# Another order table for a fused linear-attention and gated feed-forward kernel on one core

## The chip, the cores and the metric

The kernel runs on one core of a Trainium2 chip. A core has TensorE (PE, matrix products into PSUM), VectorE (DVE), ScalarE (ACT) and GpSimd (POOL), which run side by side, each through its own instructions in their order, and SyncE (SP), which issues DMAs; POOL and ACT issue DMAs as well. The metric is the device time of one execution in microseconds (us); lower is better.

## The reference

The program first does a linear attention with exponential features for 8 batches of 8 heads (576 positions, head size 64, 128 features), then a feed-forward layer over the 4608 rows of 512 that come out.

```python
def phi(x):
    proj = np.einsum('bhsd,df->bhsf', x, w_phi)
    proj = proj - np.max(np.abs(proj), axis=-1, keepdims=True)
    return np.concatenate([np.exp(proj), np.exp(-proj)], axis=-1)
q_p, k_p = (phi(q), phi(k))
kv = np.einsum('bhsf,bhsd->bhfd', k_p, v)
z = np.sum(k_p, axis=2)
num = np.einsum('bhsf,bhfd->bhsd', q_p, kv)
den = np.einsum('bhsf,bhf->bhs', q_p, z)[..., None] + 1e-06
...
x = np.ascontiguousarray(attn_out.transpose(0, 2, 1, 3)).reshape(B * S, H * D)
...
gate = np.maximum(x @ w_gate, 0.0)
val = x @ w_val
return (gate * val @ w_out).astype(np.float32)
```

## The kernel before

The work is first described as 2,077 numbered steps with their dependencies, and then issued in an order that is written out by hand as text, the table `ORDER`.

**Attention of a batch.** K is turned so that head size lies on partitions (`turn_pe` on TensorE for batches 0 and 1, `turn_dma` as a transposing DMA on SP's queue for the others). For each pair of heads (`k_item`, line 379) TensorE projects K, DVE takes the largest absolute value, ACT makes the two exponentials and the scale of each row, and POOL multiplies V by the scale (`scale`). `k_kv` (line 468) sums the products of features and scaled V in 20 small matmuls, and ACT or DVE copies the sum out ("kv copy"). For Q, `q_cols` projects, DVE takes the maximum and ACT the exponentials; `q_num` (line 585) makes numerator and denominator in three groups of heads (6, 6 and 4 matmuls), DVE combines them and takes the reciprocal, POOL divides, and the result is turned into `xT`, the feed-forward input: by TensorE with a copy by ACT or DVE for batches 0 and 1 ("xT copy"), by a transposing DMA after that. The last 64 positions of each batch are handled in pairs of batches.

**Feed-forward.** `ffn` (line 655) runs for nine groups of 512 rows: for each of 12 slices of the inner dimension, 4 matmuls with w_val, a copy by ACT, 4 matmuls with w_gate, and one DVE instruction that rectifies and multiplies. Then three times 4 matmuls with w_out for each of 4 row tiles, a copy, and a store from SP's queue. Group 0 belongs to batch 0 and is cut into parts of 128, 128 and 256 rows. Group 8 holds the left-over positions (`xT_mix`), and its last two stores are issued by ACT.

**What fixes the order.** Each entry of `ORDER` is a step's number, a letter for its engine (P for TensorE, A for ACT, D for DVE, G for POOL, S for SP) and one figure for each buffer or PSUM bank that the step is the first to use. `1397P5` issues step 1397 on TensorE and puts its result in PSUM bank 5. Some steps may run on ACT or on DVE; the letter chooses. `w21` and `z9` issue fillers (21, 9): matmuls of a zero tile that nobody reads (`warm`, line 198). Every engine runs its entries in the order of the table; semaphores enforce the dependencies. All fillers stand in the first part.

From batch 2 on, transposing DMAs (turns) and POOL's loads are kept apart: a turn waits for the last load that the table has ahead of it, and the first load after turns waits for the last turn (`read`, line 67).

```python
if o.alone and e == SP:
    o.gate, last_turn = last_load, o
if o.alone and e == POOL:
    o.gate, last_turn = last_turn, None
if o.bytes and e == POOL:
    last_load = o
```

Steps named later: 42, 196, 200 and 202 are copies of turned K (42 and 202 of the left-over rows); 98 is a kv copy and 153 an xT copy of batch 0; 270P projects Q of batch 1; 1397P and 1415P are feed-forward steps of group 0. 10S, 16G, 17G, 18G, 20G, 25G and 26G are early loads (a quarter of k; the two halves of q; two pieces of w_val; the left-over rows of v, and q, both of batch 1), 66G, 56G and 76G the scalings of V for batch 0. 711G and 1182G load v for batches 4 and 7 (711G its left-over rows), 708G left-over rows of k; 531G and 857G load left-over rows of v; 712S, 533S and 1185S turn K, 1188S turns Q, 816S turns a chunk of feed-forward input. 717P and 1190P project K of batches 4 and 7. 1983S stores a tile of group 7; 2056 is a copy of group 8, 2058S and 2069S are stores of it.

Of the kernel before, what the change touches and what calls it, by code (L numbers as in the profile page):

```python
# [1016 lines left out]
0G 4D 8S 7S 9S 1S 14S0 3D 10S 5G 6S w21 35P00 w1 33P1 13S0 36A w1 37P2 16G0 34A 2D 15S 38A w2  # L1017
57P340000 25G1 47P561111 59A 61D 67P012222 69A 48D 12S 17G 51D 11S 49A w13 41P20 22G0 68D 60A 50A
58D 18G 54A 52A w9 39P5 42D 63A 71D 23G0 w1 87P3000 40D 89A 72A 88D w8 77P25333 62A 81D 53A w4
43P40 64A 78D 74A 65A 90A 44D 91A6 73A 66G 92D 83A 93D w10 115P3 70A 116D0 79A 94D 75A w11 45P4  # L1020
84A1 80A 26G1 119P0 85D 55A 86D 108P3601 82A 56G 111A w2 103P25 105A 46D w5 113P1 112A 120D w2
134P4 104A 101P60 76G 135D1 107A 117P0 138P2 102A 114D 97P41 110A 118D 95P72 139D 21G 132P6 121A0
193P11 96A 98D 106A 127P0223 19G 133D 136P7 129A 137D 20G 109A 194D 130A z9 141P40000 29G 99P53
142D 147P61 24G1 195P7 100A 148D 131A 143D z3 144P32 122P15 196A 145D 160P41110 149D 128A 146D z3
157P21 161D 126A 197P7 150D 217P633433 158D 151G 124A 162D 154P02 159D 123A 155D z2 207P420504 198A
156D 199P1 163D 223A 218D 164G 125A 221D 220A 28G 211D z11 165P00 140A1 222A 152P7 170P50220 208D
219A 27G0 201P31 153D 200A 167P61 171D 1359P70 166A 168D 173P12 172D 31G 1360A 1363P01 169D 1375P72
174D 203P51 175D 1376A 202D 1364A 183P61010 210A 180P11 204D 247P71110 186P02 209A 1377P3 184D
1387P53 213A 187D 205P4 181D 224A 188D 212A 176D 1378D0 1361P0 177G 182D 1388A 249A 237P231015 185D
1383P52 189D 250A 206D 1365P1 190G 1385P6 1384A 243A 248D 178P5 239A 1362D z3 191P4 179D 242A  # L1030
277P70010 1366D 192D 240A 227P512220 1386D 279A 1371P40 241D 1391P61 283A 228D 1393P3 1372A 1392A
278D 1379P42 251A 252A 1373P6 254G 1380A 1374D 230A 1389P4 1394D 1381P6 232A 1390D 30G 1399P30 229A
1367P41 1382D 231D 280A 1403P53 225A 1400A 281D 1405P6 226G 234A 233A 1369P7 238D 282A 1401P3
1395P12 1404A 1402D 270P2023 1396A 1406D 1368A 1397P5 275A 1407P30 32G 1370D 1415P13 1398D 276A
271D 263P46 1416A 253G 1409P7 1408A 274D 1423P51 235A 265A 1417P1 1410D 214A 1411P32 244A 264D
1424A 236G 347P00 215A 269A 257P74 1418D 348A 1425P5 245D 1435P10 258A 1426D 1451P03 1412A 267D
273A 284P75 216G 1436A 1413P3 268A 259P15 1414D 272A 285D 1443P61 1431P32 1452A 1445P2 288D 260A
1453P0 1444A 246G 286A 1437P1 1446D 291P60 1432A 255P26 1438D 287A 292D 293D 266A 1447P31 1433P1
256D 294A 1449P7 289A 1419P40 1454D 311P60102 1434D 261P27 1448A 1420A 1450D 312D 298P01221 1421P3
262A 1455P13 290A 1422D 301P40 1459P72 313D 1456A 1457P2 302D 1471P31 1460A 299D 1461P5 300D 295P62  # L1040
1472A 1427P10 303D 296D 349P7320 1462D 1428A 297D 1429P0 1458D 350D 1463P42 308P51 304D 314P10
1430D 1464A 1465P6 305G 351A 309D 1473P2 315D 1487P43 316D 1474D 1489P0 310D 1488A 321P11012 352A
1467P20 1490D 324P50 355A 1479P41 306P71 325D 1468A 1439P03 1466D 322D 1441P2 317D 1440A 323D
1475P62 307A 318G 1442D 1469P0 327P11 1476A 1491P73 1470D 1480A 1481P2 353D 340P60222 1492A 1493P4
1477P0 328D 326D 1499P70 383G0 1494D 1482D 1495P53 329D 1478D 1483P41 1501P2 1496A 354A 356P10
1513P0 357D 358D 341D 1485P5 359A 1484A 1508P3 1500A 1486D 330D 331G 334P10 319P4 337P71 1509P 320D
381G1 335D 336D 1503P5 342D 338D 382G1 339D 366P41100 372P12 1518P6 373D 1502D 363P71 1497P2 1519P
1498D 364D 367D 1520P 343D 344G 332P2 1504P 1521A0 333D 365D 1522S 345P6 368D 1514P 346A 375P21
1539P72 386S0 376D 374D 1510P 389S0 1527P41 1505P 388S0 1528A 1540A 360P60 369P12 1506A1 1523P40
361D 387S 370D 1511A0 362D 401P753331 377D 371D 391P362122 390S 1525P2 403A 395D 394A 1515P 393A  # L1050
1507S 1524A 1512S 1535P13 1526D1 1529P4 392D 1536A 397A 411P230403 1530D 1543P10 404A 417A 405D
527G0 1541P4 378D 1544A 402D 396A 385G0 1547P11 414A 408A 431P70001 406A 1537P6 384G0 432D 1548A
1542D 1545P1 433A 532G0 434A 1531P42 1516A1 1546D 528G0 1533P7 1538D 1532A 415D 407A 421P011210
379G 1567P60 412D 416A 422D 435A 418A 529G1 413A 1549P4 409D 398A 424A 1534D 1551P53 423A 1550D
427A 468P32301 436A 447P7012 1552A 425D 437G 1553P4 452A 469D 426A 1569P5 448D 438G 473A 1568A
1555P12 472D 419A 453A 410G 1570D 1563P61 428A 450A 399D 449A 1554D 1557P5 474A 451D 1556A 400G
454P74 461P20 1558D 460A 441P18 1564A 429D 1565P5 462D 457A 420G 442A 1559P60 456A 1566D 467A
1561P1 455D 466A 533S1 458D 471A 439P59 430G 1560A 465D 443P7a 440A 380S0 459A 475P61 1576P0 476D
444A 477D 470A 1562D 482P50010 534S 479P41 463A 494P71222 445P3b 478A 483D 1577P 535S1 480D 446A
484D 464A 481D 485P10 495D 538P633534 486D 537S1 548P542025 487D 1578P 540A 488D 496D 554A 489G  # L1060
491P21 541A 1571P1 492D 1579A0 542D 490S2 509P70100 497P02 1572P 493D 543A 539D 550A 1517S 503P21
510D 1573P 498D 553A 536S 499D 551A 500D 511D 506P62 501G 504D 1581P0 544A 507D 508D 505D 518P71010
502S 515P32 512D 521P61 519D 1582P 513G 520D 516D 1574A1 674S0 558P270301 517D 522D 1583P 560A 523D
524D 549D 561A 514S 525G 568P131412 578P61110 559D 1586P5 580A 552D 526S 581A 1587P 569D 555A 562D
1580S 608P24120 570A 1588P 579D 1575S 564A 572D 563A 531G1 1599P63 582A 609D 574A 1603P72 573A
530G1 1584D0 583A 614A 1601P3 610A 709G0 575A 1607P01 1600A 707G1 545A 571A 1602D0 1605P6 1604A
710G0 1608A 1611P10 1606D 613A 585G 1613P3 556D 1612A 612D 611A 1615P73 584G 1614D 1589A1 565A
594P0630 546A 566D 1616A 601P14 615P25 598D 547G 597A 1609P3 576D 600A 1591P72 599A 1610D 621A
1595P60 567G 1592A 619D 618A 1597P3 595D 1596A 602D 620A 586P73 577G 590P60 603A 587D 596A 1623P51
616D 604A 591D 1625P7 605D 1624A 557G 1598D 592P06 607A 1593P1 606A 593D 711G0 622P60 588P57 623D  # L1070
624D 1619P30 1594D 589A 708G1 625A 632P40220 629P02 1620A 626P51 1627P12 630D 617A 627D 631D 1617P6
# [108 lines left out]
```

## Time and profile before

| | us |
|---|---|
| median of 4 runs | 385.08 |
| lowest and highest run | 383.89 and 387.73 |
| the profiled execution | 383.89 |
| its span, first to last instruction | 382.0 |
| TensorE busy | 371.1 |
| VectorE busy | 263.3 |
| ScalarE busy | 238.1 |
| GpSimd busy | 168.9 |

The profile comes from one execution. An engine's busy time counts each instant once in which one of its instructions ran; a matmul's own duration includes its way through the array, so matmuls that follow each other closely overlap. "Idle before" is the time an engine stood still ahead of an instruction, with what ended it behind an arrow. The span in 40 slices of 9.55 us, in tenths of busy time:

```profile
PE   8798999999999999999999999999999999999994
DVE  5999887558787789877976997679636745432230
ACT  5999975189978946894777478667953304122221
POOL 4885744328836943693397327813651210000000
```

The first four slices hold the attention of batch 0 and part of batch 1's, before there is much feed-forward work to run beside it. The other batches' attention lies beside the feed-forward work of the batches before, up to slice 32, and the rest is feed-forward work alone.

### The profile page before, as it was taken

The numbers are of one execution on the slowest core, as the hardware profiler recorded it, in microseconds if no ns is written. First come the engines' busy times: TensorE is split into PE (matmuls) and PEld (weight loads), VectorE is DVE, ScalarE is ACT, GpSimd is POOL, SyncE is SP. The second block draws the span as 40 slices with busy tenths as digits, with TensorE's granted clock in tenths as the row PEclk, the third lists the DMA queues.
The fourth block names the chain that finished last, engine by engine and source line by source line (L and its number), as shares of the span: only waits on it lengthen the run. The fifth ranks groups of instructions, "written<-read, shape, count | busy, mean of one in ns | idle before, by whom it ended". The sixth has DMA issues, their size and how long they took to land.

```text
span 382.0 us, 8797 instructions
## 1 busy us (share of the span) xinstructions
PE 371.1 (97%) x3376; PEld 207.3 (54%) x3376; DVE 263.3 (69%) x650; ACT 238.1 (62%) x546; POOL 168.9 (44%) x201
## 2 busy tenths in 40 slices
PE   8798999999999999999999999999999999999994
PEld 6577788544654555455546554554455544444452
DVE  5999887558787789877976997679636745432230
ACT  5999975189978946894777478667953304122221
POOL 4885744328836943693397327813651210000000
PEclk9999999999999999999999999999999999999999
DMA  8999794879746948886589559842401031200025
GB/s 211 213 137 252 111 145 58 123 143 237 113 98 184 251 91 143 164 164 106 108 227 143 83 118 202 182 87 30 124 2 44 14 57 55 70 0 0 2 82 138
DMA packets 85609, 45.00 MB, mean 118 GB/s; under 512 B 56672, under 2 KB 79072, under 8 KB 85568
## 3 DMA queue, kind: packets, MB, share of 16 engines
q0 software_dynamic: 32800, 21.83, 35.1%
q1 hardware_dynamic: 52448, 22.42, 26.1%
q8 instruction: 26, 0.43, 0.4%
q10 hardware_dynamic: 320, 0.20, 0.2%
q14 instruction: 15, 0.12, 0.1%
HBM read 37.81 MB, written 9.44 MB: 124 GB/s over the span
## 4 chain that ended last, share of the span: by engine, by line
PE 90%; DVE 3%; ACT 3%; issue 1%; DMA 1%; SPq 0%; POOL 0%; ACTq 0%; DVEq 0%; POOLq 0%
PE ps L669 48%; PE ps L707 25%; PE ps L482 5%; PE ps L600 5%; PE ps L506 2%; PE ps L389 2%; ACT kp L350 1%; DMA wo_sb<-in_k_dram 1%; ACT qp L350 1%; DVE mk L400 1%; DVE qT L328 0%; PE ps L641 0%; PE ps L436 0%; ACT kT L328 0%; PE ps L531 0%
## 5 line engine op out<-in xcount | busy, mean ns | idle before, releaser
L675 ACT CAST val<-ps 128x512 bf16<-128x512 f32 (+2 forms) x132 | 67.3, 531 | 74.2 <-PE ps L669 69.6
L678 DVE SCALAR_TENSOR_TENSOR h<-ps,val 128x512 bf16<-128x512 f32 (+2 forms) x132 | 75.4, 584 | 53.0 <-PE ps L669 38.7
L707 PE MATMUL ps<-wo_sb,h 128*128 128x512 bf16 (+1 forms) x444 | 104.3, 373 | 0.0
L669 PE MATMUL ps<-xT,wv_sb 128*128 128x512 bf16 (+2 forms) x480 | 98.9, 336 | 0.5 <-ACT xT L648 0.2
L669 PE MATMUL ps<-xT,wg_sb 128*128 128x512 bf16 (+2 forms) x480 | 99.0, 336 | 0.3 <-ACT val L675 0.3
L350 ACT ACTIVATE qp<-ps 128x512 bf16<-128x512 f32 x144 | 82.0, 631 | 9.6 <-PE ps L506 8.2
L628 POOL TENSOR_TENSOR xu<-u,r 128x512 bf16<-128x512 f32 x36 | 37.5, 1043 | 108.0 <-DVE r L625 68.8
L350 ACT ACTIVATE kp<-ps 128x512 bf16<-128x512 f32 x128 | 70.5, 616 | 5.0 <-PE ps L389 2.5
L669 PEld LDWEIGHTS <-wg_sb 128*128 128x128 bf16 x528 | 45.8, 98 | 41.5 <-issue 3.6
L669 PEld LDWEIGHTS <-wv_sb 128*128 128x128 bf16 x528 | 45.9, 98 | 40.8 <-issue 2.1
L707 PEld LDWEIGHTS <-h 128*128 128x128 bf16 x444 | 41.3, 98 | 43.4 <-issue 1.8
L415 POOL TENSOR_TENSOR vs<-vn,ek 128x1024 bf16<-128x1024 f32 x31 | 59.0, 1902 | 7.8 <-DVE ek L365 3.5
L400 DVE TENSOR_REDUCE mk<-ps 128x4 f32<-128x512 f32 x64 | 41.6, 676 | 3.7 <-PE ps L389 1.9
L516 DVE TRANSPOSE_TENSOR_REDUCE mq<-ps 128x16 f32<-128x512 f32 x56 | 37.1, 693 | 6.4 <-PE ps L506 4.4
L600 PEld LDWEIGHTS <-qp 128*128 128x128 bf16 x640 | 30.9, 98 | 16.0 <-issue 1.2
L615 DVE TENSOR_TENSOR u<-ps,t 128x195 f32<-128x195 f32 (+3 forms) x120 | 37.4, 329 | 2.0
L600 PE MATMUL ps<-kv,qp 128*128 128x65 bf16 x640 | 35.1, 193 | 0.2 <-ACT kp L350 0.2
L608 DVE TENSOR_TENSOR t<-ps,cq 128x195 f32<-128x195 f32 (+1 forms) x84 | 25.9, 325 | 13.0 <-PE ps L600 9.5
L718 ACT COPY ob<-ps 128x512 f32<-128x512 f32 x20 | 11.6, 597 | 25.6 <-PE ps L707 24.6
L482 PEld LDWEIGHTS <-kp 128*128 128x128 bf16 x512 | 21.7, 98 | 3.7 <-ACT val L675 0.4
L482 PE MATMUL ps<-vs,kp 128*128 128x65 bf16 x512 | 23.3, 193 | 0.1
L482 PE MATMUL ps<-vsm,kpm 128*128 128x65 bf16 x128 | 20.6, 193 | 0.0
(95 smaller groups left out, 317.5 us busy)
## 6 DMA issues: line engine op xcount, KB each, us to landing
out_dram<-ob SPq DMA_DIRECT2D x32, 256.0 KB, 2.5
vn<-in_v_dram POOLq DMA_DIRECT2D x7, 1024.0 KB, 8.7
kn<-in_k_dram POOLq DMA_DIRECT2D x7, 512.0 KB, 6.1
qn<-in_q_dram POOLq DMA_DIRECT2D x7, 512.0 KB, 7.1
wo_sb<-in_moe_w_out_dram POOLq DMA_DIRECT2D x1, 1536.0 KB, 13.0
wo_sb<-in_k_dram SPq DMA_DIRECT2D x4, 256.0 KB, 3.6
vn<-in_v_dram SPq DMA_DIRECT2D x4, 256.0 KB, 4.5
wg_sb<-in_moe_w_gate_dram POOLq DMA_DIRECT2D x2, 512.0 KB, 10.4
```

The costliest lines, as they stand in the source:

```text
L350: nc.scalar.activation(dst(s), ps.t.rearrange("p (c f) -> p c f", f=f), AF.Exp, scale=sign)
L400: nc.vector.tensor_reduce(m.t.rearrange("p (i x) -> p x i", x=2)[:, x], ps.t.rearrange("p (c f) -> p c f", f=F), axis=AX.X, op=ALU.max, ap ...
L415: eng.tensor_tensor(vs.t[:, :, :, 0:D], vn.t[:, 2 * u : 2 * u + 2].rearrange("p h c d -> p (h c) d")[:, :, None, :] .to_broadcast([P, 2 * ...
L482: nc.tensor.matmul(acc[:, hh, s, :], lhsT=lhsT, rhs=rhs, start=(n == 0), stop=(n == 19))
L516: nc.vector.tensor_reduce(mdst(x), ps.t.rearrange("p (h j t) -> p h j t", j=NQ, t=32), axis=AX.X, op=ALU.max, apply_absolute_value=True, a ...
L600: nc.tensor.matmul(ps.t[:, E * (2 * i + s): E * (2 * i + s + 1)], lhsT=qp.t[:, s, h, :], rhs=kv_of[b][h // 2][0].t[:, h % 2, s, :],)
L615: nc.vector.tensor_tensor(u.t[rows, lo : lo + n], ab[:, :, 0], t.t[rows, 0:n], op=ALU.add)
L628: eng.tensor_tensor(xu.t, u.t[:, :, 0:D], r.t.to_broadcast([P, H, D]), op=ALU.mult)
L669: nc.tensor.matmul(ps.t[:, 0:n], lhsT=w[:, dc, P * fi : P * fi + P], rhs=xt()[:, dc, lo:hi], start=(dc == 0), stop=(dc == NDC - 1),)
L675: nc.scalar.copy(val.t[:, 0:n], pv.t[:, 0:n])
L678: nc.vector.scalar_tensor_tensor(h.t[:, fi, lo:hi], pg.t[:, 0:n], 0.0, val.t[:, 0:n], op0=ALU.max, op1=ALU.mult,)
L707: nc.tensor.matmul(ps.t[:, lo:hi], lhsT=h.t[:, fi, P * t : P * t + P], rhs=wo_sb[:, fi, lo:hi], start=(fi == 0), stop=(fi == NFC - 1),)
```

## The change

Only the table is replaced: the same 2,077 steps in another order, with other PSUM banks and buffers, and with 87 fillers in place of 121. Of the steps that may run on either engine, 64 change it: 11 closing feed-forward copies, 9 kv copies, 8 reciprocals of scales, 3 turn copies and 2 xT copies go from ACT to DVE; 10 feed-forward copies, 8 kv copies, 10 scales, 2 turn copies and 1 xT copy go from DVE to ACT. No function changes. The new order came from two annealing passes over the author's timing model, the first for TensorE work placed in the program's early part and the second for the whole; in that model loads land sooner than they did when the old table was made.

```diff
--- before.py
+++ after.py
@@ -1014,138 +1014,138 @@
 
 
 ORDER = """
-0G 4D 8S 7S 9S 1S 14S0 3D 10S 5G 6S w21 35P00 w1 33P1 13S0 36A w1 37P2 16G0 34A 2D 15S 38A w2
-57P340000 25G1 47P561111 59A 61D 67P012222 69A 48D 12S 17G 51D 11S 49A w13 41P20 22G0 68D 60A 50A
-58D 18G 54A 52A w9 39P5 42D 63A 71D 23G0 w1 87P3000 40D 89A 72A 88D w8 77P25333 62A 81D 53A w4
-43P40 64A 78D 74A 65A 90A 44D 91A6 73A 66G 92D 83A 93D w10 115P3 70A 116D0 79A 94D 75A w11 45P4
-84A1 80A 26G1 119P0 85D 55A 86D 108P3601 82A 56G 111A w2 103P25 105A 46D w5 113P1 112A 120D w2
-134P4 104A 101P60 76G 135D1 107A 117P0 138P2 102A 114D 97P41 110A 118D 95P72 139D 21G 132P6 121A0
-193P11 96A 98D 106A 127P0223 19G 133D 136P7 129A 137D 20G 109A 194D 130A z9 141P40000 29G 99P53
-142D 147P61 24G1 195P7 100A 148D 131A 143D z3 144P32 122P15 196A 145D 160P41110 149D 128A 146D z3
-157P21 161D 126A 197P7 150D 217P633433 158D 151G 124A 162D 154P02 159D 123A 155D z2 207P420504 198A
...
-219A 27G0 201P31 153D 200A 167P61 171D 1359P70 166A 168D 173P12 172D 31G 1360A 1363P01 169D 1375P72
-174D 203P51 175D 1376A 202D 1364A 183P61010 210A 180P11 204D 247P71110 186P02 209A 1377P3 184D
...
-1395P12 1404A 1402D 270P2023 1396A 1406D 1368A 1397P5 275A 1407P30 32G 1370D 1415P13 1398D 276A
...
-624D 1619P30 1594D 589A 708G1 625A 632P40220 629P02 1620A 626P51 1627P12 630D 617A 627D 631D 1617P6
-1626D 1628A 633D 628D 644P31102 1621P2 634D 1618D 675P0730 712S0 645D 1622D 641P11 681A 638P50
...
-1085A 1021P22 1785P1 1183G1 1020D 1778A1 1103D 1060A 1046A 1780P3 1028D 1022D 1086A 1182G1 1023D
...
-1795P42 1783D1 1051A 1123A 1187S1 1799P53 1115A 1052G 1121D 1114D 1805P0 1800A 1189S1 1812A 1801P3
...
-1094A 1097P37 1032S0 1130A 1824A 1839P43 1122A 1098A 1188S 1143P01010 1131P10102 1840A 1797P5 1132D
...
-1982A0 2060P 2074D0 2061P 1997A1 1998S 2054P 2062A 2066P 2064S 2047P2 2075S 2063S 2067P 1983S 2055P
-2068D 2070A 2048P 2056A 2049P 2076A 2057S 2069S 2050A 2058S 2051S 2052S
+0G 4D 8S 7S 9S 1S 10S 3D 6S 5G w21 35P00 14S0 w1 33P1 13S0 36A w1 37P2 16G0 34A 2D 38A w2 57P340000
+17G 12S 60A 61D w2 67P561111 39P0 11S 69A 25G1 71D 41P10 15S 70A 40D 42A 72A 22G0 58D w8 47P212222
+63A 87P0000 68D 73A 20G 88D 64A 62A w7 77P56333 23G0 48D 59A w4 43P40 79A 51D 49A 26G1 81D 91A3 53A
+92D 44D 18G 54A 65A 50A 78D w14 45P4 89A 66G 94D 115P2 74A 55A 90A 93D 83A 84A0 46D 80A 75A 56G 85D
+82A w16 108P3501 116D0 97P40 52A 86D 112A 134P6 103P21 98A 111A w2 117P4 135D1 76G 113P0 106A 138P5
+118D 107A 95P61 139D 110A 136P4 119P1 96A 114D w1 101P52 109A 27G0 120D 105A 195P61 132P7 104A 137D
+127P0323 99P13 21G 121A0 102A 196D 131A 133D 141P20000 19G 193P4 100A 122P56 142D 130A 194D 147P71
+24G1 144P12 143D 128A 217P340403 148D 145D 140A1 157P21110 124A 149D 28G 146D 129A 199P7 218D
+160P11 123A 154P02 150D 158D 219A 151G 161D 159D 126A 162D z5 207P522524 155D 222A 29G 200D
...
+169D 202A 197P1 174D 153A 208D 30G z3 186P41000 203P01 198A 175D 187D 165P3 209A 211D 1383P60
...
+1397P1 244A 1400A 263P6423 1416A 245D 234A 270P07 1398D 229A 1417P3 246G 267D 276A 1411P11 1402D
...
+415D 424A 1569P4 427A 412D 437G 416A 422D 1551P51 417A 1570D 531G1 433A 1537P3 425D 1552A 423A
...
+1563P33 414A 1556A 451D 1557P2 457A 1554D 460A 1565P4 419D 428A 459A 1558D 420G 533S1 456A 468P0712
...
+588P75 607A 623D 624D 586P42 1618D 711G0 625A 1624A 590P26 589D 604A 1619P30 587A 591D 1594D
+632P61112 629P11 1620A 626P70 633D 1627P51 630D 634D 631D 675P4210 627D 712S0 638P00222 628D 677A
...
+717P520403 647D 715S 1635P43 657D 648G 1622D 723A 722A 731D 650P00 1633P6 1636A 713S 651D 733A 658D
...
+1670D 1701P2 812D 1700A 813D 797A 864P712120 856G1 1702D 808P50 866A 820P02 1683P41 821D 870A 857G1
...
+807D 823P20 1704A 1685P4 814D 868D 815G 1689P0 824D 869A 905D 825D 1695P32 907A 1690D 816S1 867A
...
+1799P40 1078A 1784S 1066A 1815P73 1800A 1090G 1108A 1113P0330 1120P64 1112A 1792P 1117D 1182G1
...
+1812A 1188S1 1795P20 1125A 1122A 1091P55 1796A 1185S1 1823P02 1098A 1092D 1130A 1123A 1095P46
...
+1840A 1133D 1119A 1145D 1134P00 1149P41 1825P1 1135D 1136D 1150D 1190P520005 1798D 1200P733530
...
+2032A 1982A0 2039P52 2044A 1983S 2041P4 2040A 2071P6 2042D 2029P1 2035P52 2030D 1996P 2046D 2036A
...
+1993S 2054P 2073P 2061P 2066P 2062A0 2067P 2074A 2055P 2063S 2076A 2075S 2068A 2048P 2064S 2070A
+2056D 2069S 2049P 2058S 2057S 2050A 2052S 2051S
```

A line of "..." marks what is left out; the whole table has 132 lines on each side.

## The prediction

> **What bounds the kernel now.** I read the page's busy shares first, then the chain of waits, then busy time by stretches, and last single instructions at the places where the new order differs.
>
> ```profile
> span 382.0 us, 8797 instructions
> PE 371.1 (97%) x3376; PEld 207.3 (54%) x3376; DVE 263.3 (69%) x650; ACT 238.1 (62%) x546; POOL 168.9 (44%) x201
> ...
> PE 90%; DVE 3%; ACT 3%; issue 1%; DMA 1%; SPq 0%; POOL 0%; ACTq 0%; DVEq 0%; POOLq 0%
> ```
>
> TensorE is busy 97% of the span and holds 90% of the chain that ended last. So a change pays only where TensorE waits, or before its first and after its last instruction. The stretches say where (columns: stretch, length, busy time and instructions of PE, PEld, DVE, ACT, POOL, granted clock, DMA share, GB/s):
>
> ```profile
> 0.00:43.60 43.60, 38.12 (x538) 30.33 (x538) 37.81 (x96) 37.72 (x94) 28.48 (x39) 1.00 1.10 190
> 43.60:377.00 333.40, 332.94 (x2841) 176.97 (x2839) 225.51 (x555) 199.91 (x454) 140.42 (x163) 1.00 0.56 108
> 377.00:382.00 5.00, 0.00 (x0) 0.00 (x0) 0.00 (x0) 0.47 (x1) 0.00 (x0) 0.95 0.51 120
> ```
>
> From 43.6 to 377 TensorE is idle for 0.46 us of 333.4: no order can win much there, and a new wait there is paid in full. After it come 5.0 us of tail. In the first 43.6 us PE's 38.1 us busy are misleading, since a short matmul counts about 0.22 us of busy time and the next follows far sooner:
>
> ```profile
> 0.99 2.42 PE L199 MATMUL ps<-zero 128*128 128x128 bf16 x21 [0.99 <-DVE zero L231]
> ...
> 7.64 0.90 PE L199 MATMUL ps<-zero 128*128 128x128 bf16 x13
> ```
>
> Thirteen filler matmuls on zeros take 0.90 us, so (0.90 - 0.22) / 12 = 0.057 us apart. I matched each engine's instructions with the table's entries in order and took the usual time from one TensorE step's start to the next: 0.22 us for a feed-forward step of width 128, 0.86 for width 512, 0.60 for a kv step, 0.19 and 0.13 for the numerator steps. With these, the steps ahead of entry 1397P, which runs at 43.6 us, come to 23.1 us, and 121 fillers x 0.057 to 6.9. The other 13.6 us TensorE waits. ACT starts its first step at 4.75 us and has 35.5 us of steps ahead of 1397P by the same measure; DVE starts at 1.1 and has 37.1. They leave 43.6 - 4.75 - 35.5 = 3.4 us of idle on ACT and 43.6 - 1.1 - 37.1 = 5.4 on DVE, most of DVE's before 7.2 us. The head is bound by ACT and DVE together.
>
> **Part 1, the head.** Entry 1397P is a fair milestone, because ahead of it TensorE has 81 steps in both tables, the same but for one: 1415P (0.22 us of feed-forward) in place of 270P (0.22 us of query projection). DVE has 84 steps instead of 86. It loses a kv copy, an xT copy and two turn copies (42, 98, 153, 202: 0.34 + 0.33 + 0.33 + 0.27 us from start to start), gains two K turn copies (196, 200: 0.33 each), and a multiply of width 128 gives way to one of 256 (+0.13): -0.5 us. ACT has 92 steps instead of 93: it takes 42, 98, 202 and 153 over (1.35 us), gives up 196 and 200 (0.93), and three steps come later (0.7 us, still to be done): -0.3 us, of which +0.4 is real extra load. Both queues are full, so I take the milestone 0.4 us earlier. From both sides: if all of ACT's 3.4 us of idle went, -3.4; if the new order left ACT and DVE 1.5 us of extra idle, as much as ACT's first wait of 1.5 us for TensorE in this trace, +1.1.
>
> Thirty-four of the 121 fillers go: 34 x 0.057 = 1.9 us of TensorE. I cost this at nothing, since they stand among 13.6 us of waiting; what follows them is released by ACT and DVE.
>
> The two rates above, 0.110 us a filler at 1 us ((2.42 - 0.22) / 20) and 0.057 at 7.6, are what the fillers are for. The Trainium skill (TensorE: Matmul & The Clock Gate, "What's actually happening") says that the array runs at half rate by default and again after an idle window of about 3.4 us; the longest PE wait here is 1.0 us, so by that rule dropping fillers costs nothing. The same page's "A second HAM failure mode: psum-queue depth-cycling" speaks against the change: frequent short idles can make the gate swing, and the sum would then be the slow rival's below. No run here shows that.
>
> **Part 2, loads.** On POOL's queue q's second half (17G) moves ahead of vm (25G), the next batch's q (26G) moves ahead of the scaling 66G, and the first two pieces of w_val (18G, 20G) change places. All weight pieces still have over 6 us of TensorE work between issue and first use, and that early a microsecond of TensorE work is well over one of time. On SP the last quarter of k (10S) moves ahead of a quarter of v. I cost these at nothing in the head; their cover is the ACT and DVE queue above, and without it a late load would cost its lateness.
>
> Later, the table holds a load closer to the transposing DMA that waits for it (turn 712S for load 711G, 1188S for 1182G), and everything behind that turn on SP's queue waits too. The tightest pairs, in TensorE work listed between them: 711G to 712S 3.1 us; 1182G to 1188S 5.6; 531G to 533S 5.6; 857G to 816S 5.7. The rows to set beside them:
>
> ```profile
> vn<-in_v_dram POOLq DMA_DIRECT2D x7, 1024.0 KB, 8.7
> kn<-in_k_dram POOLq DMA_DIRECT2D x7, 512.0 KB, 6.1
> ...
> vm<-in_v_dram POOLq DMA_DIRECT2D x14, 64.0 KB, 5.3
> ...
> kT<-kn SPq DMA_TRANSPOSE x12, 3.3
> ```
>
> By medians 711G (vm, 5.3) makes 712S 2.2 us late. Step 717P, which reads 712S, stands 4.5 us behind it; the turn lands after 3.3, so 1.2 us of slack leave 1.0 of stall. 1182G (vn, 8.7) makes 1188S 3.1 late, and 1185S behind it as much; 1190P stands 4.9 behind 1185S, so 1.6 of slack leave 1.5. Together 2.5 us, the upper end. But before has such a pair too, 708G to 712S with 3.5 us listed:
>
> ```profile
> 134.14 1.29 POOL L269 DMA_DIRECT2D vm<-in_v_dram  x2
> 135.42 1.26 POOL L269 DMA_DIRECT2D km<-in_k_dram  x2
> ...
> 138.54 1.23 SPq L337 DMA_TRANSPOSE kT<-kn  x1
> ```
>
> Load and turn are 138.54 - 135.42 = 3.1 us apart: on a queue that has drained, a small load lands in 3.1, not 5.3, and TensorE did not stop after it. 1182G too has 4.8 us of listed work between it and the load before it, and there a transfer as long is nearer to kn's 6.1: 0.5 late, inside its slack. So I take +0.3, and keep 0 to +2.5. The lower end can't be below 0 by more than the 0.46 us of idle there is.
>
> **Part 3, the tail.** Columns: start, length.
>
> ```profile
> 375.93 3.21 SPq L734 DMA_DIRECT2D out_dram<-vn  x5
> 376.89 0.59 ACT L718 COPY vn<-ps 128x512 f32<-128x512 f32 x1 [0.99 <-PE ps L707]
> ```
>
> The last copy ends at 377.48, and SP, issuing five stores back to back of some 0.6 us, reaches the last two only at 377.95. In the new table the big store 1983S comes far earlier and two of the five (2069S, 2058S) move up a place: SP should be free when the copy ends. I take -0.4 us; +0.3 if 2056, now a DVE copy of 0.69 us in place of 0.59 on ACT, holds SP instead.
>
> **Sum.** -0.4 + 0.3 - 0.4 = -0.5. The profiled run took 383.89 us with its span of 382.0, 1.9 outside the span, and would become 383.4. The median of the four runs lies 1.2 above it, so 385.08 - 0.5 = 384.6.
>
> **Rivals.** *Faster: the head's idle goes.* If annealing the early part takes out ACT's 3.4 us of idle and the tail gives 0.5, 385.08 - 3.9 = 381.2. For it: 13.6 us of TensorE waiting is the only large store of time. Against: ACT's and DVE's work ahead of the milestone is nearly unchanged, and both sit at 9.2 to 9.9 us busy in ten between 10 and 40 us. Chance 0.14.
>
> *Slower: the clock falls back in the head.* With 34 fillers fewer TensorE runs at the 0.110 us rate for part of 20 to 43.6 us. The table has 16.3 us of steps there; at half rate all of it takes 32.6, 9 us over the 23.6 there are, and half of the stretch gives about 4.5: 389.6. It decides from about 8 us at the low rate. Against: fillers at 7.6 us already run at the fast rate with TensorE no fuller than later. Chance 0.09.
>
> *Slower, loads late.* Part 2's upper end and 1.1 in the head: 385.08 + 2.5 + 1.1 - 0.4 = 388.3. For it: the table is drawn on the assumption that loads land sooner. Against: the 3.1 us pair above. Chance 0.14, half of it beyond 1%.
>
> *The order is new on paper alone:* TensorE saturated, ACT and DVE equal, 385.1. It lies inside my own case.
>
> **How the numbers follow.** My case and the paper one have 0.63. A measurement of this kernel tells about 1% (3.9 us) from no change. Faster by that: 0.14. Slower: 0.09 + 0.07 = 0.16. Within: 0.70. The range 381.6 to 388.2 takes in the bounds (-3.4 in the head, +2.5 and +1.1 for loads) and leaves out most of the clock rival and the end of the fast one.
>
> **What would show it.** Right: 1397P's matmul at about 43.2 us, PE idle under 1 us from there to the end, the last store issued at once behind the last copy. Wrong: fillers or feed-forward matmuls at twice their spacing between 15 and 45 us; PE waiting for kT near 1190P (two thirds of the span) or 717P; ACT idle of several tenths in the slices up to 40 us; or the head done more than 2 us sooner.

## The result and the profile after

The kernel with the new order takes 386.86 us (median of 43 runs, 384.78 to 391.1) against 385.25 for the kernel before (64 runs): ratio 1.0051, with an interval of 1.0037 to 1.0065. By the ratio it is 2.0 us slower, by the medians 1.6: inside the range of the prediction, but on the other side of no change from its 384.6. Ratios leave out executions more than 1.5% above the fastest of their kernel, medians and mean clocks do not (one of the new order's, and in the table of experiments one of fill34's and three of q26's). The profiled execution took 387.33 us, its span is 385.5. First the page, its span, TensorE's busy share and the shares of the chain that ended last:

```profile
span 385.5 us, 8716 instructions
...
PE 371.1 (96%) x3342; PEld 206.9 (54%) x3342; DVE 263.5 (68%) x652; ACT 234.8 (61%) x544; POOL 169.1 (44%) x201
...
PE 72%; DVE 9%; ACT 8%; DMA 5%; issue 3%; POOL 2%; SPq 1%; POOLq 0%; DVEq 0%; ACTq 0%
```

TensorE's busy time is the same 371.1 us, but its share of the chain fell from 90% to 72%: the work now waits for other engines. The stretches (same columns as before) show where:

```profile
43.60:377.00 333.40, 329.82 (x2820) 175.18 (x2818) 225.99 (x556) 196.10 (x446) 138.16 (x160) 1.00 0.54 106
```

Behind the head TensorE is idle for 333.40 - 329.82 = 3.6 us; before it was 0.46. The timeline names two places. ACT first (start, length, in brackets the idle before and what ended it), then TensorE:

```profile
190.26 0.59 ACT L718 COPY ob<-ps 128x512 f32<-128x512 f32 x1 [2.62 <-DMA out_dram<-ob]
...
244.19 0.59 ACT L718 COPY ob<-ps 128x512 f32<-128x512 f32 x1 [3.55 <-DMA out_dram<-ob]
```

```profile
190.90 1.09 PE L506 MATMUL ps<-qT,w 64*128 64x512 bf16 x4 [0.58 <-ACT ob L718]
244.83 1.02 PE L669 MATMUL ps<-xT,wg_sb 128*128 128x512 bf16 x4 [1.70 <-ACT ob L718]
```

These are the copies of a feed-forward row tile into an output buffer, steps 1710A and 1793A. There are two such buffers (`ob`), and each copy waits until the store that still reads its buffer has landed. While ACT waits, everything behind the copy on its queue waits, and then TensorE. Issue and landing from the trace's DMA records: store 1658S, which 1710A waits for, is issued only at 187.56 us, behind the turns 816S, 1000S and 863S on SP's queue, and lands at 190.19; store 1784S, which 1793A waits for, is issued at 238.00 and lands at 244.10, 6.1 us later, while the median store takes 2.6. Four of POOL's loads (1179G to 1182G) are on their way beside it.

I matched the entries of the tables with the traces again and took the time at which each order reaches the same amount of TensorE work, in us against the kernel before:

| reached by the kernel before at | new order | ob3 | store190 | ob3fill18 | new601fill |
|---|---|---|---|---|---|
| 43.6 | -0.81 | +2.28 | -0.04 | -1.30 | -1.42 |
| 186.3 | -0.96 | +2.05 | -0.61 | -2.42 | -2.39 |
| 206.7 | +0.32 | +2.10 | -0.57 | -2.37 | -1.87 |
| 227.5 | +0.43 | +2.64 | +0.43 | -0.60 | -1.87 |
| 248.2 | +2.94 | +2.90 | +6.73 | -0.48 | -1.55 |
| 375.8 | +3.06 | +3.47 | +6.85 | -0.44 | -1.55 |

(The other columns are experiments below.) The new order is 1 us ahead up to 186 us, loses 1.3 near 190 and 2.5 near 244. In the tail the stores bunch:

```profile
377.14 5.52 SPq L734 DMA_DIRECT2D out_dram<-vn  x8
```

All eight of SP's stores of the last group go out back to back, since the group's first copy (2062A) now starts at 376.53 us, 3.4 us before TensorE's last matmul ends; before, the first one (2074D) started at 369.97, 6.9 us ahead of that end. From TensorE's last matmul to the end of the span it takes 385.5 - 379.9 = 5.6 us, before 5.15.

One more thing is seen in no single profile. Over all its executions the kernel before has a mean granted clock of 0.998, the new order one of 0.993. In the 17 of its executions with a clock of 0.996 or more the new order takes 386.2 us on average, 0.8 more than the kernel before over all its executions (385.4); the slowest, 391.1 us, has 0.985. So there are two questions: what the waits cost, and what the clock costs. They can't be split by the clock alone, since the clock drops in long waits of TensorE, as the traces below show.

### The profile page after: what moved, and what is told of

Same layout as the page of the kernel before. It is cut to its first block, busy times and chain, and to the rows that moved or that the text cites. A ratio compares the mean times of both kernels' runs of the same rounds, so it can differ in the third digit from the quotient of the medians.

```text
span 385.5 us, 8716 instructions
## 1 busy us (share of the span) xinstructions
PE 371.1 (96%) x3342; PEld 206.9 (54%) x3342; DVE 263.5 (68%) x652; ACT 234.8 (61%) x544; POOL 169.1 (44%) x201
## 4 chain that ended last, share of the span: by engine, by line
PE 72%; DVE 9%; ACT 8%; DMA 5%; issue 3%; POOL 2%; SPq 1%; POOLq 0%; DVEq 0%; ACTq 0%
PE ps L669 41%; PE ps L707 18%; PE ps L482 4%; PE ps L600 4%; ACT kp L350 3%; DMA out_dram<-ob 3%; ACT qp L350 2%; DVE h L678 2%; DVE u L615 2%; DVE mk L400 2%; PE ps L506 2%; DVE t L608 2%; DMA wo_sb<-in_k_dram 1%; PE ps L389 1%; PE ps L321 1%
## 5 line engine op out<-in xcount | busy, mean ns | idle before, releaser
L675 ACT CAST val<-ps 128x512 bf16<-128x512 f32 (+2 forms) x132 | 68.4, 551 | 81.6 <-PE ps L669 76.5
L669 PE MATMUL ps<-xT,wg_sb 128*128 128x512 bf16 (+2 forms) x480 | 97.5, 336 | 2.0 <-ACT ob L718 1.7
L669 PE MATMUL ps<-xT,wv_sb 128*128 128x512 bf16 (+2 forms) x480 | 97.7, 336 | 0.6 <-ACT ekm L363 0.4
L350 ACT ACTIVATE qp<-ps 128x512 bf16<-128x512 f32 x144 | 83.7, 665 | 4.7 <-PE ps L506 2.5
L350 ACT ACTIVATE kp<-ps 128x512 bf16<-128x512 f32 x128 | 73.4, 637 | 12.2 <-PE ps L389 10.6
L669 PEld LDWEIGHTS <-wg_sb 128*128 128x128 bf16 x528 | 45.9, 98 | 42.9 <-issue 3.5
L600 PEld LDWEIGHTS <-qp 128*128 128x128 bf16 x640 | 30.0, 98 | 14.3 <-issue 1.8
L600 PE MATMUL ps<-kv,qp 128*128 128x65 bf16 x640 | 34.1, 193 | 0.5 <-ACT kp L350 0.3
L718 ACT COPY ob<-ps 128x512 f32<-128x512 f32 x18 | 10.6, 591 | 17.4 <-PE ps L707 10.0
```

The costliest lines, as they stand in the source:

```text
L350: nc.scalar.activation(dst(s), ps.t.rearrange("p (c f) -> p c f", f=f), AF.Exp, scale=sign)
L600: nc.tensor.matmul(ps.t[:, E * (2 * i + s): E * (2 * i + s + 1)], lhsT=qp.t[:, s, h, :], rhs=kv_of[b][h // 2][0].t[:, h % 2, s, :],)
L669: nc.tensor.matmul(ps.t[:, 0:n], lhsT=w[:, dc, P * fi : P * fi + P], rhs=xt()[:, dc, lo:hi], start=(dc == 0), stop=(dc == NDC - 1),)
L675: nc.scalar.copy(val.t[:, 0:n], pv.t[:, 0:n])
```

## The experiments

All ratios are against runs of the kernel before on the same chip; 'clock' is the mean granted clock of all executions.

| run | what differs from the new order | median us | ratio [interval] | clock |
|---|---|---|---|---|
| ob3 | 3 output buffers, 10 kv tiles | 386.24 | 1.0028 [1.0002, 1.0054] | 0.991 |
| swap243 | buffers and stores near 244 us exchanged | 387.30 | 1.0056 [1.0027, 1.0086] | 0.992 |
| store190 | store 1658S ahead of three turns | 387.81 | 1.0068 [1.0037, 1.0099] | 0.991 |
| loads243 | two loads away from store 1784S | 391.03 (one execution) | - | 0.984 |
| tail | last ten TensorE steps reordered | 387.25 | 1.0045 [1.0014, 1.0076] | 0.994 |
| fill34 | 34 fillers more | 390.21 | 1.0092 [1.0058, 1.0125] | 0.997 |
| fill18 | 18 fillers more | 388.25 | 1.0078 [1.0050, 1.0105] | 0.995 |
| q26 | load 26G put back | 389.58 | 1.0057 [1.0025, 1.0089] | 0.991 |
| ob3fill | 3 buffers, 34 fillers more | 385.69 | 0.9999 [0.9968, 1.0029] | 0.998 |
| ob3fill18 | 3 buffers, 18 fillers more | 385.68 | 1.0003 [0.9983, 1.0023] | 0.996 |
| newhead | old order behind 1397P | 385.57 | 1.0004 [0.9976, 1.0032] | 0.992 |
| oldhead | old order up to 1397P | 392.06 | 1.0151 [1.0095, 1.0207] | 0.995 |
| new601 | old order behind 601P | 383.62 | 0.9957 [0.9929, 0.9984] | 0.991 |
| new601fill | the same, 18 fillers more | 382.62 | 0.9944 [0.9920, 0.9967] | 0.997 |
| best1397 | newhead, 18 fillers more, 26G back | 384.78 | 0.9991 [0.9969, 1.0012] | 0.998 |
| best601 | new601fill, 26G back | 382.18 | 0.9923 [0.9901, 0.9944] | 0.998 |
| turns227 | ob3fill18, load 1036G behind 1039S | 392.33 | 1.0181 [1.0153, 1.0209] | 0.983 |
| turnsonly | load 1036G behind 1039S | 396.02 | 1.0262 [1.0220, 1.0303] | 0.980 |

### The output buffers

```diff
-        "ob": ring("ob", 2, [P, DM], FP32),
+        "ob": ring("ob", 3, [P, DM], FP32),
-        "kv": ring("kv", 12, [P, 2, 2, E]),
+        "kv": ring("kv", 10, [P, 2, 2, E]),
 ORDER
- 1516D1 ... 1783A1 ...
+ 1516D2 ... 1783A2 ...
```

> The new order, but with three output buffers (ob) instead of two, handed out in turn; kv tiles go from 12 to 10 to make room. Nothing else moves. Theory, the output buffers: after the head the new order loses about 4.1 us, and most of it where a copy into ob waits for the store that still reads that buffer (ACT idle 2.62 us at 190 and 3.55 at 244). With a third buffer those waits go, TensorE's idle between 43.6 and 377 us falls from 3.6 us to under 1, and the time falls by 2 to 3.5 us, to a ratio of 0.996 to 1.000 against the kernel before. Rival, the loads: if TensorE is late because loads and the transposes behind them land late, a buffer more changes nothing: ratio 1.004 to 1.007, TensorE's idle still above 3 us. Rival, the head or the clock: the same, 1.004 to 1.007.

No copy waits for a store any more, and TensorE's idle behind the head falls from 3.6 to 2.35 us (the expectation had under 1); the table of progress shows a loss of 0.05 us near 190 and 0.3 near 244, where the new order lost 1.3 and 2.5. But the time fell by 0.2% only, the intervals of the two ratios overlap, and this profile's head is 3.1 us later than the new order's. Its timeline and its stretches (the last three figures are granted clock, DMA share and GB/s) show why:

```profile
13.16 0.62 PE L321 MATMUL ps<-ident,qn 128*128 128x128 bf16 x8 [1.57 <-DMA qn<-in_q_dram]
13.62 0.94 PE L199 MATMUL ps<-zero 128*128 128x128 bf16 x14
16.69 1.03 PE L321 MATMUL ps<-ident,qn 128*128 128x128 bf16 x8 [2.13 <-DMA qn<-in_q_dram]
```

```profile
43.60:377.00 333.40, 331.05 (x2850) 177.29 (x2849) 229.08 (x563) 198.45 (x457) 140.18 (x163) 1.00 0.55 107
...
14.00:16.00 2.00, 0.56 (x11) 0.39 (x7) 1.96 (x5) 2.00 (x8) 0.29 (x1) 0.91 1.52 232
16.00:18.00 2.00, 1.31 (x11) 1.19 (x12) 0.97 (x3) 1.43 (x4) 1.05 (x2) 0.50 1.45 198
18.00:20.00 2.00, 2.00 (x19) 1.70 (x17) 2.00 (x4) 0.00 (x0) 2.00 (x3) 0.50 1.63 185
20.00:22.00 2.00, 2.00 (x26) 1.26 (x24) 0.39 (x2) 0.95 (x3) 2.00 (x3) 0.50 1.47 198
```

TensorE waits 1.57 and 2.13 us for q; inside the second wait, at about 15.6 us, the clock falls to 0.50, and it stays there for over 6 us. That is the second question, the clock, taken up below.

```diff
- 1788D0 1180G0 ... 1793A1 ...
+ 1788D0 1789S 1180G0 ... 1793A0 ...
```

> The new order with two edits around 243 us: store 1789S goes ahead of 1784S on SP's queue, and copies 1793A and all later ones change their ob buffer (0 for 1, 1 for 0), so that 1793A waits for 1789S instead of 1784S. Theory, the output buffers: 1793A's wait of 3.55 us falls to under 2 us, since its buffer's store is issued 1.7 us sooner; TensorE's idle of 1.70 us in front of 1805P goes or falls below 0.5, and the time falls by 1 to 2.4 us: ratio 0.999 to 1.003. The stall at 190 us stays. Rival, the loads: 1805P is late whatever the buffer; ratio 1.004 to 1.007.

The wait of 1793A fell from 3.55 to 2.76 us, TensorE's from 1.70 to 0.92, and the time did not fall. The store that 1793A now waits for, 1789S, went out sooner, but took 7.0 us beside the same loads: exchanging the buffers exchanged the slow store.

```diff
- 1657D0 1677P7 862S1 ... 863S ... 838D 1658S
+ 1657D0 1658S 1677P7 862S1 ... 863S ... 838D
```

> The new order with one edit: store 1658S goes right behind the copy that it stores (1657D), ahead of turns 816S, 1000S and 863S on SP's queue. Theory, the place on SP's queue: the store is issued some 6 us before 187.56, copy 1710A no longer waits 2.62 us for it, TensorE's stall at 190.9 us goes, and the time falls by 0.5 to 1.3 us: ratio 1.002 to 1.004. The stall at 243 us stays. Rival, the loads: the store's place matters nothing, ratio 1.004 to 1.007.

The mechanism held: 1658S landed at 173.7 us, 1710A started 1.15 us after its predecessor for TensorE's sake and not for the store, and the progress table shows no loss near 190 (-0.61 to -0.57). The time got no better, because TensorE then came to 244 us with the same slow store ahead of it, and paid more:

```profile
245.55 0.58 ACT L718 COPY ob<-ps 128x512 f32<-128x512 f32 x1 [4.92 <-DMA out_dram<-ob]
```

```profile
244.00:246.00 2.00, 0.00 (x0) 0.00 (x0) 0.00 (x0) 0.45 (x1) 1.49 (x2) 0.81 0.95 308
246.00:248.00 2.00, 1.81 (x7) 0.71 (x7) 1.33 (x3) 1.69 (x5) 0.45 (x1) 0.50 0.41 162
248.00:250.00 2.00, 2.00 (x24) 1.40 (x22) 0.72 (x2) 1.75 (x5) 2.00 (x2) 0.50 0.02 4
250.00:252.00 2.00, 2.00 (x7) 0.84 (x5) 0.85 (x3) 0.00 (x0) 0.65 (x2) 0.50 1.01 198
```

TensorE waits 3.07 us for this copy and is idle for the whole of 244 to 246 us, and from about 245.2 on the clock stands at 0.50 for over 6 us. The stall thus costs twice its length: the progress table loses 6.3.

```diff
- 1074D 1181G1 1790P2 ... 1788D0 1180G0 1111A ... 1182G1 1110D 1803P52 1121D 1089G 1793A1
+ 1074D 1790P2 ... 1788D0 1111A ... 1182G1 1110D 1803P52 1121D 1089G 1181G1 1180G0 1793A1
```

> The new order with loads 1181G and 1180G put behind 1182G and 1089G on POOL's queue, so that they no longer lie beside store 1784S; the stores and the output buffers are as they were. Theory, the store is slow because loads lie beside it: 1784S, which took 6.1 us from issue to landing (238.0 to 244.1) with three loads in flight, lands in 3 to 4 us, and the wait of copy 1793A falls from 3.55 us to under 1.5. Rival, the store is slow of itself or for its place on SP's queue: still 5.5 to 6.5 us.

Store 1784S landed 4.5 us after its issue: neither 3 to 4 nor 5.5 to 6.5. In this one execution, then, the two loads that moved away account for part of the 6.1 us; 1179G and 1182G were still there. The copy's wait fell to 1.97 us. But the moved loads hold up the turns behind them, and TensorE pays there:

```profile
259.29 0.62 PE L389 MATMUL ps<-w,kT 64*128 64x128 bf16 x16 [2.34 <-DMA kT<-kn]
```

### Fillers and the clock

```diff
- w4 43P40 ... w14 45P4 ... 152P60
+ w4 w12 43P40 ... w14 w14 45P4 ... w8 152P60
```

> The new order with 34 fillers more (12 ahead of 43P, 14 ahead of 45P, 8 ahead of 152P), so 121 in all as before; nothing else moves. They stand where TensorE waits in the head for q's transposes and for the first xT turn. In the runs so far the kernel before has a mean granted clock of 0.998, kernels with the new head 0.991 to 0.994, and their times follow the clock by about 2 to 2.5 us per 0.01. Theory, fewer fillers let the clock drop in the head of some executions: mean clock back to 0.996 or more, time 0.5 to 1.5 us shorter than the new order, ratio 1.001 to 1.004. Rival, the clock drops for the waits themselves (late q loads) and fillers do not help: mean clock 0.991 to 0.994, ratio 1.004 to 1.007. Rival, fillers in a saturated head cost time: 34 x 0.057 = 1.9 us more, ratio 1.008 to 1.011.

> Three output buffers (kv tiles 10 instead of 12) and the 34 fillers back, in the new order. Theory, the two causes are the copies that wait for an output buffer and the clock in the head, and they add: mean clock 0.996 or more, no wait of a copy for a store, ratio 0.996 to 0.999. Rival, the fillers do nothing: 1.000 to 1.005, as with three buffers alone (1.0028). Rival, fillers cost time: above 1.005.

In these two the 8 fillers ahead of 152P write into a PSUM bank that holds a step's result, so that a part of the first batch's attention comes out changed; the amount of work is the same. The clock came back to 0.997 and 0.998, as the theory had it. The time did not follow in the new order (1.0092, inside the range of the rival that has fillers cost time); with three buffers it came to 0.9999, 3.6 us less. So fillers hold the clock, but with two output buffers the new order gains nothing by it. The next two say the same with fewer fillers, and with those ahead of 152P in a bank that is free:

```diff
- w4 43P40 ... w14 45P4 ... 152P60
+ w4 w6 43P40 ... w14 w6 45P4 ... z6 152P60
```

> The new order with 18 fillers more and nothing else: 6 each ahead of 43P, 45P and 152P. Theory, two losses that feed each other: the head's clock holds with them, but the stall near 244 us stays and drops the clock there in some executions: mean clock 0.994 to 0.998, ratio 1.002 to 1.006. Rival, the clock in the head is all of the loss: mean clock 0.997 or more and a ratio of 0.996 to 1.000. Rival, fillers shift the head and everything behind it comes late, as with 34: 1.007 or more.

> The new order throughout, with three output buffers (kv tiles 10 instead of 12) and 18 fillers more. Theory, output buffers and the clock are the two large losses of the new order: with both gone the head's gain is left, less the bunched stores of the tail: mean clock 0.997 or more, ratio 0.994 to 0.998. Rival, late loads between 60 and 260 us cost as much: 0.999 to 1.004.

fill18 fell out with the third rival (1.0078), ob3fill18 with its rival, late loads (1.0003). Between the two lie 0.75%, 2.9 us, for one output buffer more. What is left shows in fill18's timeline of TensorE and in its stretches:

```profile
221.23 1.04 PE L389 MATMUL ps<-w,kT 64*128 64x128 bf16 x16 [2.26 <-DMA kT<-kn]
```

```profile
218.00:220.00 2.00, 0.97 (x5) 0.24 (x3) 2.00 (x6) 0.21 (x1) 0.15 (x1) 1.00 1.64 109
220.00:222.00 2.00, 0.77 (x16) 0.77 (x16) 0.44 (x1) 0.12 (x1) 0.00 (x0) 0.75 0.62 122
222.00:224.00 2.00, 2.00 (x12) 0.71 (x7) 0.69 (x1) 2.00 (x5) 0.00 (x0) 0.50 0.55 105
224.00:226.00 2.00, 2.00 (x15) 1.04 (x14) 1.49 (x4) 1.34 (x3) 0.09 (x1) 0.89 0.98 191
```

Step 1053P waits for turn 1038S (K of batch 6). In the new table the 1 MB load 1036G stands ahead of this turn and of 1042S and 963S, and turns wait for the last load ahead of them: 1036G landed at 213.7 us, 1042S was issued at 213.8, and 1038S came to land at 221.2. In the new order's own profile 1038S landed 0.28 us before 1053P, which came later there; in ob3fill18 1053P waited 1.6 us. A TensorE that is ahead runs into this load, and in fill18 the wait again drops the clock. Part of the lateness is the turn's own: 1038S took 4.7 us from issue to landing in fill18 and ob3fill18, but 3.3 in the new order's profile; why stays open.

```diff
- 43P40 79A 51D 49A 26G1 81D ... 89A 66G 94D
+ 43P40 79A 51D 49A 81D ... 89A 66G 26G1 94D
```

> The new order with one load put back: 26G, the next batch's q, goes behind the scaling 66G on POOL's queue, as in the old order. In the old order q's second half (17G) landed at 14.8 us, in the kernels with the new head at 15.4 to 16.7, since 26G is issued at 13 us while it is on its way. Theory, the load moved ahead makes q late, and the wait for q lets the clock drop: 17G lands at 14.5 to 15.4, TensorE's waits for q in front of 43P and 45P shrink by 0.5 to 1.5 us, mean clock 0.995 or more, ratio 1.002 to 1.005. Rival, 26G does not matter: 17G at 15.4 to 16.7, clock 0.991 to 0.994, ratio 1.004 to 1.007.

The rival was right: q's second half (17G) landed at 16.3 us with 26G out of its way, no sooner than in the other new heads (15.1 to 16.8), and the clock stayed at 0.991. In the profile of oldhead, which has the old head, 17G landed at 17.0 us. So the later q is not shown to come from the new order at all: what spreads its landing from 14.8 to 17.0 us stays open.

Nor does the length of a wait alone decide whether the clock drops. Below are eight matmuls of one kind behind a wait for q, first from q26's profile and then from that of the run tail:

```profile
13.01 1.04 PE L321 MATMUL ps<-ident,qn 128*128 128x128 bf16 x8 [1.81 <-DMA qn<-in_q_dram]
```

```profile
16.74 0.62 PE L321 MATMUL ps<-ident,qn 128*128 128x128 bf16 x8 [2.63 <-DMA qn<-in_q_dram]
```

In q26 the clock has dropped during the shorter wait (0.62 on average from 12 to 14 us) and the matmuls take 1.04 us; in tail it stays at 1.00 through the longer one and they take 0.62.

```diff
- 1036G0 929A ... 992D 1039S 989D
+ 929A ... 992D 1039S 1036G0 989D
```

> The new order with three output buffers and 18 fillers more (ratio 1.0003 so far) and one edit: load 1036G (1 MB of v) goes behind turn 1039S, so that turns 1042S, 963S, 1038S and 1039S no longer wait for it. In the run without the edit 1036G landed at 211.7, turn 1038S was issued at 214.4 and landed at 219.2, and 1053P, which reads it, waited 1.6 us for it. Theory, late loads: 1038S lands 3 us or more sooner, 1053P does not wait, the time falls by 1 to 1.8 us: ratio 0.995 to 0.998. Rival, v is now late in its turn (vs 1062G near 234 us): 0.999 to 1.004.

> The new order with the same single edit, load 1036G behind turn 1039S, and nothing else. Theory, in the new order alone TensorE comes to 1053P later and 1038S is seldom late (0.28 us of slack in its profile), and the output buffers' stall near 244 us takes what is won: ratio 1.002 to 1.005. Rival, the late load is the main loss of the new order in most executions: 0.997 to 1.001.

Both missed. In turns227, in an execution whose clock had dropped in the head too, turn 1038S landed 2.4 us sooner (216.8) and 1053P did not wait. But 1036G now waits for turn 1039S, lands at 227.8, and the turns behind it, 1040S and 1041S, wait for it in their place. TensorE pays for 1041S in turns227's timeline:

```profile
232.41 0.61 PE L506 MATMUL ps<-qT,w 64*128 64x512 bf16 x2 [7.61 <-DMA qT<-qn]
```

A load can't be moved through a run of turns, only in front of it or behind it. What the late load is worth in a typical execution of the new order is therefore not measured by itself.

### The head, the rest and the tail

newhead keeps the new order up to 1397P and issues what is left in the old order; oldhead does the reverse; new601 has the seam at 601P, at about 125 us, where what the two orders have ahead of the seam differs by four entries (three in the new order alone, one in the old). At the seams:

```diff
 newhead
- 1397P1 244A 1400A 263P6423 1416A
+ 1397P1 229A 1400A 234A 1402D 270P2023
 new601
- 601P52 617A 1595P73 595D 618A
+ 601P52 556D 598D 547G 597A 1609P3
```

> The new order up to 1397P with its 87 fillers, and from there all that is left in the old order (a few PSUM banks, val and qp slots change). Theory: the head alone gains about 1 us where its clock holds, and loses it where the clock drops; the old order behind it has no wait for output buffers. So mean clock 0.991 to 0.995 and a ratio of 0.998 to 1.003; a profiled execution at full clock has TensorE's progress 0.5 to 1.5 us ahead of the kernel before from 60 to 350 us. Rival, the loss sits in the head alone: ratio 1.004 to 1.006.

> The old order up to 1397P with its 121 fillers, and from there all that is left in the new order. Theory: the clock holds (mean 0.996 or more), the copies wait for output buffers near 190 and 244 us, and the tail's stores bunch: ratio 1.003 to 1.008. Rival, the loss sits in the head alone: ratio 0.998 to 1.001.

> The new order up to 601P (about 125 us) with its 87 fillers, the old order behind it, nothing else. Theory: the order behind 601P costs the new kernel 3 to 4 us (output buffers and what follows from them), so without it, but with the head's clock dropping in some executions: mean clock 0.991 to 0.995, ratio 0.994 to 0.998. Rival, the fillers and 26G made the gain of the same kernel with both: 1.000 or more.

newhead and new601 fell as the theory had it, and new601 is the main reading: with the old order behind 601P the ratio goes from 1.0051 to 0.9957. Everything that the new order loses, 0.94% or 3.6 us, it loses behind 601P; what it does ahead of it is worth 0.43% or 1.7 us, clock and all. This gain is not the head's alone: with the seam at 1397P nothing of it can be told from zero (newhead, 1.0004). oldhead is slower than either kernel by more than any theory had (1.0151); that the part behind the head does not stand a head that is 0.9 us later is a guess. Its profile, with 388.7 us the fastest of its six executions, shows TensorE waiting 1.1 us for scaled V at 131 us and 1.1 for kT at 223, and a copy waiting 2.0 for its output buffer at 245; what the slower ones add stays open.

> As new601 with the 18 fillers; 26G stays where the new order has it. Theory: the clock holds, mean 0.997 or more, and the time is as with 26G put back: ratio 0.991 to 0.994, 382 to 383 us. Rival, 26G's place mattered: 0.995 to 0.999. Rival, the six executions of that kernel were a lucky draw: 0.996 or more.

> The new order up to 1397P, the old order behind it, with 26G behind 66G and 18 fillers more (6 each ahead of 43P, 45P and 152P). Theory: the new head's gain with its clock held. The new head in front of the old order took 384.64 us in the executions with a clock of 0.996 or more, against 385.42 for the kernel before; so with the clock at 0.996 to 0.998 the ratio is 0.997 to 0.999. Rival, fillers and the later load cost what the clock gives back: 0.999 to 1.002.

> The same with the seam at 601P instead of 1397P, where the two orders differ by three entries: the new order up to about 125 us, the old one behind it, 26G behind 66G, 18 fillers more. Theory: nothing is lost up to 160 us in the new order's profile, so this keeps the head's gain without the 1.5 us lost behind the seam at 1397P: ratio 0.996 to 0.998. Rival, the new order's loads between 60 and 110 us land too late in some executions: 0.999 to 1.005.

Their edits are those shown, put together. The clock of the head in new601's profile and then in new601fill's, first 43.6 us each:

```profile
0.00:43.60 43.60, 36.62 (x478) 29.71 (x479) 34.38 (x89) 34.76 (x86) 28.82 (x39) 0.88 1.12 192
```

```profile
0.00:43.60 43.60, 37.33 (x534) 30.36 (x535) 37.84 (x97) 38.02 (x99) 31.46 (x44) 1.00 1.18 201
```

With 18 fillers the clock stays at 1.00, and entry 1397P, or the same amount of work, is reached 3.6 us sooner than in that execution without them (42.2 and 45.8 us). Over all executions the difference is smaller, 383.6 to 382.6 us, since the clock does not drop in each, and the intervals overlap. Nor do 18 fillers rule a drop out: in best601's profile the clock stands at 0.50 from 29.0 to 32.4 us. best601 is the fastest kernel, 0.9923: 3.0 us faster than the kernel before and 1.3% faster than the new order. Its interval overlaps with new601fill's, so 26G's place is not shown to matter. Its page:

```profile
span 381.2 us, 8744 instructions
...
PE 369.3 (97%) x3360; PEld 207.9 (55%) x3360; DVE 264.5 (69%) x656; ACT 233.7 (61%) x540; POOL 169.1 (44%) x201
```

```diff
- 2053P2 ... 2060P ... 2054P 2073P 2061P 2066P 2067P 2055P 2048P 2049P
+ 2053P2 ... 2060P ... 2061P 2073P 2066P 2067P 2054P 2055P 2048P 2049P
```

> The new order with TensorE's last ten steps in another order, so that the third row block of the last group is summed first (2053 2060 2061 2073 2066 2067 2054 2055 2048 2049); copies and stores keep their order. Theory, the stores of the tail bunch: copy 2062A ends about 1.3 us sooner, the eight stores on SP start at about 375.9 instead of 377.14 and are through before the last copy, and the end is set by that copy and its two stores: the span falls by 0.4 to 0.8 us, ratio 1.003 to 1.004. Rival, the tail is set by TensorE's last step and the last transfer alone: no change, ratio 1.005.

The times can't tell it (1.0045 beside 1.0051), the trace can: from TensorE's last matmul to the end it takes 385.6 - 381.0 = 4.6 us instead of 5.6, since SP is through with the earlier stores when the last copy ends. So the bunched stores cost the new order's tail some 1 us. TensorE itself ended 1.1 us later in this execution, which hides it in the span.

## Why the prediction was wrong

**What bounds the kernel: right.** Behind the head a new wait is paid in full: TensorE's idle there rose by 3.1 us, and that is most of the 4.0 us that the progress table loses behind 186 us.

**Part 1, the head: right in sign in the profile, but the fillers were not free.** In the profile 1397P came 0.6 us sooner (43.0 for 43.6; forecast 0.4), in new601fill's, with 18 fillers more, 1.2; in new601's, where the clock dropped, it came at 45.9. One step that failed is 'I cost this at nothing', of the 34 fillers, and its reason, that the longest wait of TensorE in the trace of before is 1.0 us. With the new head and its fewer fillers the waits for q are longer, up to 2.76 us (new601), and in some executions the clock drops in them. The cover that I named, ACT and DVE as the bound, hides the fillers' own time, but not what the fillers are for. The clock rival had this mechanism with 4.5 us. Where it strikes it costs nearly that, 3.6 us between the profiles of new601 and new601fill; in the mean the two kernels differ by 0.5 to 1 us, and their intervals overlap. The two sections of the Trainium skill that the prediction weighed (TensorE: Matmul & The Clock Gate, "What's actually happening" and "A second HAM failure mode: psum-queue depth-cycling") point both ways: the idle window of about 3.4 us spoke for no cost, the warning of frequent short idles against the change. The runs show drops inside single waits that are shorter than that window, 1.81 us (q26) and 2.26 us (fill18), and none in one of 2.63 us (tail); here the measurement decides, and what tells the waits apart is not shown.

**The sum: a term is missing, and it turned the sign.** Parts 1 to 3 go through loads, turns and the tail's stores. The 32 stores of output tiles between are costed nowhere: neither their place on SP's queue, which I counted for turns alone, nor the two buffers that they hold. In the new table three of group 4's four copies use buffer 1, and 1658S stands behind three turns; both could be read from the tables. The order behind 601P, priced at 0.3 us for loads and -0.4 for the tail, costs 3.6 us. With three buffers the waits for stores are gone. That is worth 2.9 us with 18 fillers more (fill18 to ob3fill18) and 0.9 us without them (1.0051 to 1.0028, where the intervals overlap). What ob3fill18 still loses against new601fill, 0.59% or 2.3 us, no experiment takes apart; its trace shows the wait of 1.6 us for 1038S.

**Part 2, late loads: right in kind, wrong in place.** None of the four pairs that I listed stopped TensorE in the profile. The pair that counts, 1036G ahead of 1042S and 1038S, I did not list: I measured the distance from each load to the first turn behind it in TensorE work, and not how late a turn further back on the queue then is. Its cost is hidden in the profile and 1.6 to 2.3 us where the head is ahead (ob3fill18, fill18). That loads slow down stores was not thought of.

**Part 3, the tail: forecast -0.4, measured +0.45** (5.6 for 5.15). I looked at SP's last two stores and not at when the first copy of the group comes.

**What the chances came to.** That the time lies inside the stated range is luck in part: a gain of 1.7 us ahead of 601P and a loss of 3.6 us behind it make up the 2.0 us, and neither has the size or the cause that the sum gave it. The two slower rivals were each half right, the clock in the head and late loads; the waits for output stores were in none of them.

## What to carry over

Behind every copy into a small ring stands the transfer that frees it. When an order is changed, follow stores from copy to landing as one follows loads: their place on the issuing queue, what lies beside them, and who is next for their buffer. On an engine that is saturated, a stall of 2 us is not worth 2 us if the clock drops after it, so fillers are judged by the waits of the new order, over several executions, and not by those of the old one; and an order should be judged part by part, since here its first third was a gain and the rest a loss.

## What the runs showed of the hardware

A store of 256 KB, 2.5 us from issue to landing in the median, took 6.1 to 7.5 us beside three or four loads of up to 1 MB (1784S in the new order and store190, 1789S in swap243), and 4.5 in one execution with two of them moved away (loads243). The granted clock fell to 0.50 inside waits of TensorE, 1.1 us into one of 2.13 (ob3), 1.3 into one of 1.81 (q26) and 2.0 into one of 2.26 (fill18), but not in waits of 2.48 (best1397) and 2.63 us (tail). Ahead of the tail it then stood at 0.50 for 3.4 us (fill18), 6.8 (ob3, store190) or 10.2 (turns227), though TensorE had work again. 18 fillers of 0.06 us each, put ahead of the waits, brought the mean clock of new601 from 0.991 to 0.997.
